# Reordering eighteen passes over six token units, with plain products in the first passes

## The chip, the cores and the metric

One Trainium2 chip, of which the kernel uses one core. A core has five engines that run beside each other, each through its own list of instructions in order: TensorE (PE) for matrix products, VectorE (DVE) and ScalarE (ACT) for element work, GpSimd (POOL), and SyncE (SP), whose list here only issues DMA transfers. The metric is device time in microseconds of the kernel's one core; lower is better.

## The reference

Attention with a mask that keeps the first `n_global` keys and the last `n_local` positions of each query, followed by a gated projection. Everything is float32, and the kernel has to match it to float32 accuracy.

```python
B, H, S, D = 4, 8, 768, 64          # n_global 8, n_local 96
scores = q @ k.T / sqrt(D)
keep = is_global | is_local
scores += -slope[h] * dist          # slope 2**-(h+1); dist = n_local for global keys
a = softmax(where(keep, scores, -1e9))
x = (a @ v)                         # reshaped to 3072 tokens x 512
out = ((x @ w_a) * (x @ w_b)) @ w_out   # w_a, w_b: 512 x 1536; w_out: 1536 x 512
```

## The kernel before, in words

**Units and granules.** The 3,072 tokens are cut into six units of 512 tokens (`NU`). Attention of a unit is four granules (`granule_ops`), one for each pair of heads. A granule loads a tile `qk` and a tile `vt`, has PE make the scores of its four blocks of 128 queries into PSUM banks `ps` (L544), lets DVE add the mask and take the maximum (L559), ACT the exponentials (L575), and DVE or ACT the division (L615, L612). The probabilities are then turned: for unit 0 by PE through the banks `pt` (`direct`), for the others by DVE in 32 x 32 squares into `tt` (L634), which goes by DMA to a DRAM tile `mir` and comes back in eight strided reads into `px` and `py` (`carry`). PE multiplies them with `vt` into a bank `pa` (L648), and ACT copies that to a quarter of the unit's tile `x` (tag `X`, one buffer).

**Passes.** The 1,536 columns of `w_a` and `w_b` are cut into six blocks of 256 (index `fp`, 0 to 5), and two blocks make a weight set: set A is `fp` 0 and 1, B is 2 and 3, C is 4 and 5. A pass is one set on one unit, and there are 18. `PASSES` (L48) orders them: A over units 0 to 5, B over 5 to 0, C over 0 to 5. A pass has two half passes, one for each `fp`. `project` makes the two products of a half pass by Strassen's scheme with seven products of 2 x 2 halves (`product`, L809, banks `al` and `ga`), each of 12 matmuls of 256 columns: a float32 factor is split in a high part `H` and a low part `L`, and three of the four cross products are taken. The products need seven forms of the weights (`FORMS`) and seven of `x` (`XFORMS`, made by `forms`): sums and differences of quarters, each then split by a cast and a subtraction (`split`, L299/L301 and L309). `back` (L907) multiplies the result, split into `hh` and `hl`, with the two blocks of `w_out` (`w_O`) into four PSUM banks `acc`, with 24 matmuls of 512 columns. The half passes overlap: PE does `back` of one between the products of later ones. When the unit changes, `evict` adds `acc` to what DRAM holds of that unit (`part`, through the tile `o`, three buffers) and stores it again, or to the output.

**Weights.** They arrive as 64-bit words and are made float32 by `to32`, six tiles for each `fp` (`wr<-wts`, then two ACT and four DVE instructions into `wm`). Set A is made straight into its SBUF slots (`direct`); sets B and C are made beside earlier passes, saved to DRAM (`dw<-wm`), and loaded and split into the slots when the set changes (`load_w`, `wl<-dw`). There are slots for one set only. The tile `x` of a unit is saved too (`dx<-x`) and loaded again for its later passes (`xl<-dx`).

**What sets the order.** Nothing here is placed by hand. Each instruction is an `Op` with a due time, the buffers it reads and writes, and a cost on each engine that may do it. `Schedule.order` runs a list schedule over these costs (earliest due time first among what is ready and has its buffers) and the instructions are emitted in the resulting order on each engine. `run` gives the due times: `times` are the starts of the passes, and the attention of a unit is spread from one and a half passes to half a pass ahead of its first use, so unit 1 has the first half of pass 0, and units 2 to 5 one pass each, up to the middle of pass 4. All DMAs go through SP's queue, in order.

## Time and profile before

| what | us |
|---|---|
| median of three runs (lowest, highest) | 773.75 (771.92, 776.95) |
| the profiled execution, its own time | 777.12 |
| its span (first to last instruction) | 775.3 |
| PE, DVE, ACT busy | 699.4, 579.0, 372.0 |
| moved by DMA | 149.55 MB, mean 193 GB/s |

In the profile's groups of instructions each row gives the line, the engine, the operation, the tile written and those read, and the count. The view by windows gives busy time of each engine in each stretch of the span, the share of full speed at which TensorE's clock was granted, the mean busy share of the 16 DMA engines and the rate. The view of instructions in order of time merges neighbours of a kind (`x12`); a row's duration contains the pipeline's depth, so the cost of one of several in a row is the distance between starts. In slices of a fortieth of the span (19.4 us), the DMA engines are at eight or nine tenths from the fifth to the nineteenth, and PE is at nine tenths without a break from the 20th to the 39th.

### The profile page before, as it was taken

The numbers are of one execution on the slowest core, as the hardware profiler recorded it, in microseconds if no ns is written. First come the engines' busy times: TensorE is split into PE (matmuls) and PEld (weight loads), VectorE is DVE, ScalarE is ACT, GpSimd is POOL, SyncE is SP. The second block draws the span as 40 slices with busy tenths as digits, with TensorE's granted clock in tenths as the row PEclk, the third lists the DMA queues.
The fourth block names the chain that finished last, engine by engine and source line by source line (L and its number), as shares of the span: only waits on it lengthen the run. The fifth ranks groups of instructions, "written<-read, shape, count | busy, mean of one in ns | idle before, by whom it ended". The sixth has DMA issues, their size and how long they took to land.

```text
span 775.3 us, 13998 instructions
## 1 busy us (share of the span) xinstructions
PE 699.4 (90%) x5104; PEld 633.3 (82%) x5104; DVE 579.0 (75%) x1610; ACT 372.0 (48%) x937; POOL 1.7 (0%) x8
## 2 busy tenths in 40 slices
PE   3875868989998979996999999999999999999993
PEld 3755756988887968886999999999999999999992
DVE  4799899988978767877998876757657567575551
ACT  2886686656567656654654623223434132232310
POOL 0000000000000000000000000000000000000000
PEclk9996999999999999999999999999999999999997
DMA  5664888999999989888574733314522232142031
GB/s 197 251 230 161 246 250 300 304 298 304 286 299 288 295 250 308 280 273 309 189 236 163 253 133 119 109 55 164 172 92 70 90 124 98 66 164 82 28 109 72
DMA packets 64093, 149.55 MB, mean 193 GB/s; under 512 B 7440, under 2 KB 26000, under 8 KB 61968
## 3 DMA queue, kind: packets, MB, share of 16 engines
q1 hardware_dynamic: 64016, 148.57, 57.3%
q8 instruction: 42, 0.69, 0.4%
q14 instruction: 35, 0.29, 0.1%
HBM read 100.31 MB, written 48.23 MB: 192 GB/s over the span
## 4 chain that ended last, share of the span: by engine, by line
PE 61%; DMA 19%; DVE 13%; ACT 3%; SPq 2%; issue 2%; DVEq 0%; ACTq 0%
PE al L809 20%; PE acc L907 20%; PE ga L809 15%; DMA mir<-tt 7%; DMA wr<-wts 5%; DMA qk<-qk 4%; PE pa L648 3%; PE ps L544 3%; DVE tt L634 2%; SPq L290 2%; DVE t L559 2%; DMA py<-mir 1%; ACT t L575 1%; DVE t L615 1%; DVE xf_T L309 1%
## 5 line engine op out<-in xcount | busy, mean ns | idle before, releaser
L907 PE MATMUL acc<-w_O,hh 128*128 128x512 f32 x576 | 197.9, 403 | 0.0
L809 PE MATMUL al<-xf_T,w_S 128*128 128x256 f32 x864 | 119.8, 288 | 12.1 <-ACT w_S L299 6.1
L907 PEld LDWEIGHTS acc<-w_O,hh 128*128 128x128 f32 x576 | 108.5, 188 | 23.1 <-issue 0.3
L809 PEld LDWEIGHTS al<-xf_T,w_S 128*128 128x128 f32 x864 | 110.9, 194 | 15.5 <-ACT s L299 7.0
L907 PE MATMUL acc<-w_O,hl 128*128 128x512 f32 x288 | 113.8, 395 | 0.2 <-DVE hl L309 0.2
L575 ACT ACTIVATE t<-t,sm 128x168 f32<-128x168 f32 x192 | 81.9, 428 | 50.4 <-DVE sm L559 50.2
L544 PE MATMUL ps<-qk 128*128 128x168 f32 x384 | 76.6, 329 | 28.5 <-DMA qk<-qk 18.3
L299 ACT COPY s<-al 128x512 f32<-128x512 f32 x71 | 41.6, 586 | 110.8 <-PE al L809 110.5
L544 PEld LDWEIGHTS ps<-qk 128*128 128x128 f32 x384 | 60.4, 199 | 38.3 <-DVE sm L559 15.0
L559 DVE CUSTOM_DVE_ANT_0 t<-ps,mask 128x168 f32<-128x168 f32 x192 | 57.0, 326 | 23.2 <-PE ps L544 23.1
L299 ACT CAST hh<-h 128x512 fp32r<-128x512 f32 x60 | 36.9, 619 | 63.5 <-DVE h L309 38.2
L809 PE MATMUL ga<-xf_B,w_A 128*128 128x256 f32 x432 | 59.8, 288 | 4.7 <-ACT xf_B L299 2.6
L838 DVE TENSOR_TENSOR s<-ga,s 128x512 f32<-128x512 f32 x72 | 49.6, 688 | 19.0 <-PE ga L809 18.5
L907 PEld LDWEIGHTS acc<-w_O,hl 128*128 128x128 f32 x288 | 54.3, 189 | 10.3 <-DVE hl L309 0.6
L809 PE MATMUL ga<-xf_B,w_S 128*128 128x256 f32 x432 | 58.1, 283 | 2.0 <-ACT s L299 1.8
L809 PEld LDWEIGHTS ga<-xf_B,w_A 128*128 128x128 f32 x432 | 55.2, 192 | 5.8 <-ACT xf_B L299 3.1
L809 PE MATMUL ga<-xf_T,w_S 128*128 128x256 f32 x432 | 58.5, 284 | 1.2 <-DVE w_S L309 1.2
L809 PEld LDWEIGHTS al<-xf_B,w_A 128*128 128x128 f32 x432 | 56.7, 192 | 3.2 <-DVE w_A L309 0.5
L809 PE MATMUL al<-xf_B,w_A 128*128 128x256 f32 x432 | 58.8, 285 | 0.3 <-DVE w_A L309 0.3
L809 PE MATMUL al<-xf_T,w_A 128*128 128x256 f32 x432 | 57.7, 282 | 0.4 <-DVE s L838 0.4
L809 PEld LDWEIGHTS ga<-xf_B,w_S 128*128 128x128 f32 x432 | 53.6, 188 | 3.4 <-ACT s L299 3.1
L809 PEld LDWEIGHTS al<-xf_T,w_A 128*128 128x128 f32 x432 | 54.4, 188 | 2.4 <-DVE s L838 1.4
(97 smaller groups left out, 1024.3 us busy)
## 6 DMA issues: line engine op xcount, KB each, us to landing
qk<-qk SPq DMA_DIRECT2D x24, 976.0 KB
wr<-wts SPq DMA_DIRECT2D x36, 512.0 KB
mir<-tt SPq DMA_DIRECT2D x20, 768.0 KB
vt<-vd SPq DMA_DIRECT2D x24, 512.0 KB
part<-o SPq DMA_DIRECT2D x40, 256.0 KB
xl<-dx SPq DMA_DIRECT2D x10, 1024.0 KB
o<-part SPq DMA_DIRECT2D x40, 256.0 KB
px<-mir SPq DMA_DIRECT2D x60, 128.0 KB
```

The lines of the kernel that those rows point to most:

```text
L290: lambda e: self.nc.sync.dma_start(out(), src()),
L299: self.nc.scalar.copy(out(), src())
L309: lambda e: self.nc.vector.tensor_tensor(out(), a(), b(), op=op),
L544: nc.tensor.matmul(ps[:, s * KW : s * KW + KW], qk[:, (2 * i + s) * P : (2 * i + s) * P + P], qk[:, k0 : k0 + KW], start=True, stop=True, ...
L559: lambda e, i=i, w=w, ps=ps, j=j, kind=kind: nc.vector.tensor_tensor_reduce(t[:, i, w], ps[:, w], self.mask[p][:, kind, w], -0.125, 3.0e38 ...
L575: lambda e, i=i, w=w, j=j: nc.scalar.activation(t[:, i, w], t[:, i, w], AF.Exp, bias=sm[:, 0, j : j + 1], scale=-1.0, accum_out=sm[:, 1, j ...
L615: nc.vector.tensor_scalar(flat()[:, j], flat()[:, j], sm[:, 3, j : j + 1], None, op0=ALU.mult)
L634: nc.vector.transpose(dst[:, s, b, e0 : e0 + n], src)
L648: nc.tensor.matmul(pa[64 * h : 64 * h + 64, i * P : i * P + P], vt[:lanes, v0 : v0 + 64], k[:, 2 * h : 2 * h + 2, :, i].rearrange("p g s k ...
L809: self.nc.tensor.matmul(bank[:, ab * HT : ab * HT + HT], w[:, a, (2 * ab + c) * P : (2 * ab + c) * P + P], x[:, b, c], start=first, stop=F ...
L838: lambda e: nc.vector.tensor_tensor(s[:, :], bank[:, :], s[:, :], op=ALU.add),
L907: self.nc.tensor.matmul(acc[i][:, :], a[:, rows], w[:, b], start=first and f == 0 and k == 0, stop=False, skip_group_check=True,)
```

## The change

- **Order of the passes.** A over units 0, 1, 2; B over 2, 1, 0; C over 0 to 5; B over 5, 4, 3; A over 3, 4, 5. The set changes four times in place of two, so B and A are loaded twice, and A's seven forms are made a second time from the input (`CONV`: `fp` 0 and 1 in passes 8 to 13) and saved to DRAM.
- **Attention.** Unit 1 keeps the first half of pass 0 and unit 2 its one pass; units 3, 4 and 5 have two and a half passes each, passes 2.5 to 10 (`SPANS`). Their result goes from the bank `pa` into the granule's own tile `vt` and from there to DRAM (`dx`), not into `X`, and `load_x` fetches it.
- **Plain products in passes 0 to 2** (`STD`, set A on units 0, 1, 2). `convert_plain` makes the four quarters and the two `w_out` blocks of set A without sums or differences; `plain_forms` splits the four quarters of `x` as they are; `project_plain` makes four products of 12 matmuls of 512 columns, the second of each two multiplied by DVE into `h`. The half passes of these three passes have 48 matmuls of 512 columns in place of 84 of 256.
- **Early slots.** The plain products leave six slots of set A unused; the first six forms of `fp` 2 are split into them while A is in use (`spread`, `slot`, `self.early`), and `load_w` skips these. The other forms of the first load of B rotate through the rest.
- **Start.** The two first `qk` tiles, the position table and the slopes are fetched ahead of the branch on the flag, into tiles outside the pools (`build`).
- **End.** The last pass loads its four old `part` blocks into the quarters of `X` and adds there (`close`), in place of the three `o` buffers.

The engines' lists show it at three places. The first is the end of SP's list, the last transfers of the program; `o` is the tile in which the old sum and `acc` are added, `part` the old sum in DRAM. Before:

```order
L290 DMA o_2_678611_8453<-part_2_349150_5078 128x512
L290 DMA out<-o_0_678611_8389 128x512
L290 DMA out<-o_1_678611_8393 128x512
L290 DMA out<-o_2_678611_8453 128x512
L290 DMA o_3_678611_8525<-part_3_349150_5104 128x512
L290 DMA out<-o_3_678611_8525 128x512
```

After, from the same kind of place:

```order
L301 DMA X<-part_2_542676_6922 128x512
L301 DMA X<-part_3_542676_6961 128x512
L301 DMA out<-o_0_666063_7959 128x512
L301 DMA out<-o_1_666063_7962 128x512
L301 DMA out<-o_2_666063_8024 128x512
L301 DMA o_3_666063_8258<-part_3_573523_7325 128x512
L301 DMA out<-o_3_666063_8258 128x512
L301 DMA out<-X 128x512 x4
```

The load of the fourth block stood behind the store of the last unit's third; now all four loads stand ahead of the previous unit's stores.

The second is PE's list at the first half pass, after the last granule of unit 0. Before:

```order
L809 MATMUL ga_0_624<-xf_B_40000_608,w_A_584 128x256 x12
L809 MATMUL al_0_546<-xf_T_40000_622,w_S_671 128x256 x12
L809 MATMUL al_0_546<-xf_T_40000_645,w_S_665 128x256 x12
L544 MATMUL ps_1_0_725<-qk_1_444 128x168 x2
L809 MATMUL ga_0_624<-xf_T_40000_480,w_S_658 128x256 x12
L809 MATMUL ga_0_624<-xf_B_40000_612,w_S_692 128x256 x12
```

After:

```order
L880 MATMUL al_0_0_593<-xp_0_313,w_A_0_499 128x512 x3
L880 MATMUL al_0_0_593<-xp_1_448,w_A_0_499 128x512 x3
L880 MATMUL al_0_0_593<-xp_2_565,w_A_0_539 128x512 x3
L880 MATMUL al_0_0_593<-xp_3_581,w_A_0_539 128x512 x3
L880 MATMUL ga_0_0_620<-xp_0_313,w_A_0_499 128x512 x3
L880 MATMUL ga_0_0_620<-xp_1_448,w_A_0_499 128x512 x3
```

The products read the quarters `xp` and `w_A` themselves; the sums and differences `xf_T` and `w_S` are gone from here.

The third is PE's list at the start of the pass of set B over unit 0, where the number after `al` or `ga` is that of the pass. Before (pass 11):

```order
L809 MATMUL al11_2_6242<-xf0_B11_450114_6093,w2_A11_288999_4087 128x256 x12
L809 MATMUL ga11_2_6255<-xf0_B21_450114_6111,w2_A12_288999_4182 128x256 x12
L809 MATMUL al11_2_6242<-xf0_T2_450114_6134,w2_S2_288999_4212 128x256 x12
L809 MATMUL ga11_2_6255<-xf0_T1_450114_6154,w2_S1_288999_4255 128x256 x12
L809 MATMUL al11_2_6242<-xf0_T3_450114_6193,w2_S3_288999_4321 128x256 x12
```

After (pass 5):

```order
L564 MATMUL ps4_0_0_3208<-qk0_78 128x168 x2
L861 MATMUL al5_2_3215<-xf0_B11_243959_3019,w2_A11_0_1236 128x256 x12
L861 MATMUL ga5_2_3231<-xf0_B21_243959_3091,w2_A12_0_1337 128x256 x12
L861 MATMUL al5_2_3215<-xf0_T2_243959_3111,w2_S2_0_1658 128x256 x12
L564 MATMUL ps4_0_1_3283<-qk0_78 128x168 x2
L861 MATMUL ga5_2_3231<-xf0_T1_243959_3137,w2_S1_0_1639 128x256 x12
L861 MATMUL al5_2_3215<-xf0_T3_243959_3270,w2_S3_0_1644 128x256 x12
L668 MATMUL pa3_3_3332<-px0_212,vt3_3_2749 64x128 x2
```

A pass that had products alone now has scores of unit 4 (`ps4_0`) and values of unit 3 (`pa3_3`) between them.

The diff, cut to its core:

```diff
-PASSES = [(0, u) for u in range(NU)] + [(1, u) for u in reversed(range(NU))] + [
-    (2, u) for u in range(NU)
-]
+ORDER = ((0, (0, 1, 2)), (1, (2, 1, 0)), (2, (0, 1, 2, 3, 4, 5)), (1, (5, 4, 3)), (0, (3, 4, 5)))
+PASSES = [(g, u) for g, us in ORDER for u in us]
+SPANS = {1: (0.0, 0.5), 2: (0.5, 1.5), 3: (2.5, 5.0), 4: (5.0, 7.5), 5: (7.5, 10.0)}
+NEAR = (0, 1, 2)
+CONV = {2: (0.8, 1.8), 3: (1.8, 2.8), 4: (3.2, 4.4), 5: (4.4, 5.6), 0: (8.0, 10.5), 1: (10.5, 13.0)}
+STD = tuple((0, u) for u in NEAR)
+PLAIN = ("A11", "A12", "A21", "A22")
+SLOT = {"A21": "S3"}
+XTAGS = ("B11", "B21", "B22", "T1")
...
+    def spread(self):
+        lead = FORMS[:6]
+        for k, name in enumerate(lead):
+            self.places[2, name] = f"w{k // 3}_" + ("S1", "S2", "S4")[k % 3]
+        rest = [(2, n) for n in ("A22", "O0", "O1")] + [(3, n) for n in FORMS + ("O0", "O1")]
+        free = [(f, n) for f in range(2) for n in ("A11", "A12", "S3", "A22", "O0", "O1")]
+        for (fp, name), (f, n) in zip(rest, free):
+            self.places[fp, name] = f"w{f}_{n}"
+        return [(2, name) for name in lead]
+
+    def slot(self, fp, name, due):
+        tag = self.places.get((fp, name)) or self.places.get((fp - 2, name))
+        tag = tag or f"w{fp % 2}_{SLOT.get(name, name)}"
+        self.places[fp, name] = tag
+        w = self.plan.buf(self.wp, [P, 2, CN], F32R, tag, f"w{fp}_{name}_{due:.0f}")
+        self.w[fp, name] = w
+        return w
+
     def wform(self, fp, name, due, src, direct):
-        if direct:
-            w = self.plan.buf(self.wp, [P, 2, CN], F32R, f"w{fp % 2}_{name}", f"w{fp}_{name}")
-            self.w[fp, name] = w
+        if direct or (fp, name) in self.early:
+            due += 0.0 if direct else 500.0
+            w = self.slot(fp, name, 0.0)
             self.split(due, lambda: src[:, :], w, lambda: w[:, 1], lambda: w[:, 0], CN, [src])
-            return
+            if direct:
+                return
...
+    def convert_plain(self, fp, due, step):
+        for i, name in enumerate(PLAIN + ("O0", "O1")):
+            m = self.to32(fp, i, due + i * step, "m" + (PLAIN + ("S1",))[i % 5])
+            self.wform(fp, name, due + i * step, m, True)
+
     def load_w(self, fp, due, step):
         for j, name in enumerate(FORMS + ("O0", "O1")):
+            if (fp, name) in self.early:
+                self.early.remove((fp, name))
+                continue
             at = due + j * step
-            w = self.plan.buf(
-                self.wp, [P, 2, CN], F32R, f"w{fp % 2}_{name}", f"w{fp}_{name}_{due:.0f}"
-            )
-            self.w[fp, name] = w
+            w = self.slot(fp, name, due)
...
+            self.copy(due + VLAG, lambda: x[:, p], lambda: pa[:, :], T, [pa], [(x, p)], psum=True)
+            return
+        self.copy(due + VLAG, lambda: vt[:, :T], lambda: pa[:, :], T, [pa], [vt], psum=True)
+        self.dma(
+            due + VLAG,
+            lambda: d[:, p * T : p * T + T],
+            lambda: vt[:, :T],
+            [vt],
+            [(d, p)],
+            T * 4 * P,
+        )
...
-        x = self.sbuf([P, NPAIR, T], F32, "X", f"x{u}", XBUFS)
+        if u in NEAR:
+            x = self.kept("X", f"x{u}")
+            for p in range(NPAIR):
+                self.granule_ops(u, p, t0 + (t1 - t0) * p / NPAIR, x)
+            return x
+        d = self.dram([P, NPAIR * T], F32, f"dx{u}")
+        self.xsaved[u] = d
         for p in range(NPAIR):
-            self.granule_ops(u, p, t0 + (t1 - t0) * p / NPAIR, x)
-        return x
+            self.granule_ops(u, p, t0 + (t1 - t0) * p / NPAIR, None, d)
...
+    def plain_forms(self, u, due, x):
+        done = []
+        for p in range(NPAIR):
+            f = self.sbuf([P, 2, T], F32R, "x_" + XTAGS[p], f"xp{u}_{p}")
+            self.split(
+                due,
+                lambda p=p: x[:, p],
+                f,
+                lambda f=f: f[:, 1],
+                lambda f=f: f[:, 0],
+                T,
+                [(x, p)],
+            )
+            done.append(f)
+        return done
...
+    def plain_product(self, due, bank, ws, k, x):
+        def emit(e):
+            for p in range(NPAIR):
+                w = ws[p // 2]
+                for a, b in ((0, 0), (0, 1), (1, 0)):
+                    self.nc.tensor.matmul(
+                        bank[:, :],
+                        w[:, a, (2 * k + p % 2) * P : (2 * k + p % 2) * P + P],
+                        x[p][:, b],
+                        start=p == 0 and a + b == 0,
+                        stop=False,
+                        skip_group_check=True,
+                    )
+
+        reads = [(b, h) for b in list(ws) + list(x) for h in "HL"]
+        self.plan.op(due, emit, reads, [bank], pe=12 * pe(T))
+
+    def project_plain(self, i, fp, due, x):
+        n = f"{i}_{fp}"
+        st = 12 * pe(T)
+        parts = []
+        for f in range(2):
+            ws = [self.w[fp, PLAIN[2 * f + c]] for c in range(2)]
+            al, ga = self.bank("al", f"al{n}_{f}"), self.bank("ga", f"ga{n}_{f}")
+            s = self.sbuf([P, T], F32, "s", f"s{n}_{f}", 3)
+            h = self.sbuf([P, T], F32, "h", f"h{n}_{f}", 2)
+            t = due + 2 * f * st
+            self.plain_product(t, al, ws, 0, x)
+            self.copy(
+                t + st, lambda s=s: s[:, :], lambda al=al: al[:, :], T, [al], [s], psum=True
+            )
+            self.plain_product(t + st, ga, ws, 1, x)
+            self.plan.op(
+                t + 2 * st,
+                lambda e, h=h, ga=ga, s=s: self.nc.vector.tensor_tensor(
+                    h[:, :], ga[:, :], s[:, :], op=ALU.mult
+                ),
+                [ga, s],
+                [(h, 0), (h, 1)],
+                dve=dve(T),
+            )
+            parts.append(self.cut(t + 2 * st, n, f, h))
+        return parts
...
+    def close(self, u, due, i, acc, o):
+        old = self.part[u, i]
+        self.dma(
+            due - 9000.0, lambda: o[:, i], lambda: old[:, :], [old], [(o, i)], 512 * 4 * P
+        )
+        self.plan.op(
+            due,
+            lambda e: self.nc.vector.tensor_tensor(o[:, i], acc[:, :], o[:, i], op=ALU.add),
+            [acc],
+            [(o, i)],
+            dve=dve(512),
+        )
+        r = u * T + i * P
+        self.dma(due, lambda: self.out[r : r + P], lambda: o[:, i], [(o, i)], [], 512 * 4 * P)
...
+        self.early = self.spread()
         self.masks()
         self.zeros()
         events = []
         x0 = self.attention(0, 0.0, START - ATT0)
-        self.convert(0, START - CONV0, STEP0, True)
+        self.convert_plain(0, START - CONV0, STEP0)
         self.save_x(0, START, x0)
-        xf = {0: self.forms(0, START - FORM0, x0)}
-        self.convert(1, START + CONV1, 2500.0, True)
-        live = None
+        xf = {0: self.plain_forms(0, START - FORM0, x0)}
+        self.convert_plain(1, START + CONV1, 2500.0)
         prev = None
         for i, (s, u) in enumerate(PASSES):
             t = times[i]
             if i and PASSES[i - 1][1] != u:
                 if events and events[0][0] == u:
-                    xf[u] = self.forms(u, t - 7000.0, events.pop(0)[1])
+                    x = events.pop(0)[1]
+                    xf[u] = (self.plain_forms if (s, u) in STD else self.forms)(u, t - 7000.0, x)
                 else:
                     xf[u] = self.load_x(u, t - 7000.0)
-            for v, (a, b) in span.items():
+            elif i and PASSES[i - 1] in STD and (s, u) not in STD:
+                xf[u] = self.forms(u, t - 7000.0, x)
...
+            for fp, (a, b) in CONV.items():
+                if i <= a < i + 1:
+                    self.convert(fp, at(a), (at(b) - at(a)) / 6, False)
...
+        tiles["X"] = cp.tile([P, NPAIR, T], F32, name="X")
+        width = 8 * KW
+        nc.sync.dma_start(tiles["qk0"], a["qk"][0, 0])
+        nc.sync.dma_start(
+            tiles["X"].rearrange("p a b -> p (a b)")[:, :width], a["pos"][:, :width]
+        )
+        nc.sync.dma_start(tiles["slope"], a["pos"][:, width:])
+        nc.sync.dma_start(tiles["qk1"], a["qk"][0, 1])
```

More of the change, by code (lines that the diff above doesn't have):

```diff
@@ L261, with __init__ @@
 class Fast:
-    def __init__(self, ctx, tc, a, out, nf, ident):
+    def __init__(self, ctx, tc, a, out, nf, ident, tiles=()):
         self.tc, self.nc = tc, tc.nc
@@ L265, in __init__ @@
         self.ctx = ctx
+        self.tiles = dict(tiles)
+        self.places = {}
         self.plan = Schedule()
@@ L451, in masks @@
         n = 2 * 2 * KW
[L452 to L453 removed]
+        full = self.kept("X", "tab")
+        self.slope = self.kept("slope", "slope")
         self.mask = [self.sbuf([P, 2, 2 * KW], F32, f"mask{p}", f"mask{p}") for p in range(1, 5)]
[L455 to L470 removed]
         part = lambda i: full[:, :].rearrange("p a b -> p (a b)")[:, i * n : i * n + n]
@@ L511, in zeros, with granule_ops @@
                 )
[L513 removed]
+    def granule_ops(self, u, p, due, x, d=None):
         nc, op = self.nc, self.plan.op
@@ L894, in project @@
         )
-        return [finish(due + 8 * st, f) for f in range(2)]
+        return [self.cut(due + 8 * st, n, f, h[f]) for f in range(2)]
     def back(self, fp, due, parts, acc, first):
@@ L922, in back, with evict @@
                 )
-    def evict(self, u, due, acc, first, last):
+    def evict(self, u, due, acc, first, last, final):
+        end = self.kept("X", f"end{due:.0f}") if final else None
         for i in range(4):
+            if final:
+                self.close(u, due, i, acc[i], end)
+                continue
             o = self.sbuf([P, 512], F32, "o", f"o{u}_{i}_{due:.0f}", 3)
@@ L960, in run @@
         fpt = 7 * 12 * pe(HT) + 24 * pe(512)
+        more = 12 * pe(HT)
         att = 4 * NPAIR * (2 * 620.0 + 530.0) / 2 * 1.0 + 600.0
-        first_use, last_use, seen = {}, {}, set()
+        last_use, seen = {}, set()
         for i, (s, u) in enumerate(PASSES):
-            first_use.setdefault(u, i)
             last_use[u] = i
         share = [0.0] * len(PASSES)
-        span = {}
-        prev = 0
-        for u in sorted(first_use, key=first_use.get):
-            if not first_use[u]:
-                continue
-            span[u] = None
-        for u in span:
-            span[u] = (max(first_use[u] - 1.0 - AHEAD, 0.0), first_use[u] - AHEAD)
-        for u, (a, b) in span.items():
+        for u, (a, b) in SPANS.items():
             for i in range(len(PASSES)):
@@ L979, in run @@
         for i in range(len(PASSES)):
-            times.append(times[-1] + 2 * fpt + share[i])
+            times.append(times[-1] + 2 * fpt + share[i] + (2 * more if PASSES[i] in STD else 0.0))
         def at(pos):
@@ L1026, in run @@
                 due = t + k * (times[i + 1] - t) / 2
-                parts = self.project(i, fp, due, xf[u])
+                plain = (s, u) in STD
+                parts = (self.project_plain if plain else self.project)(i, fp, due, xf[u])
                 if prev:
-                    prev(due + 84 * pe(HT))
+                    prev(due + (96 if plain else 84) * pe(HT))
                 over = k == 1 and (i + 1 == len(PASSES) or PASSES[i + 1][1] != u)
@@ L1034, in prev @@
                     if over:
-                        self.evict(u, d + 24 * pe(512), acc, u not in seen, i == last_use[u])
+                        self.evict(u, d + 24 * pe(512), acc, u not in seen, i == last_use[u], i + 1 == len(PASSES))
                         seen.add(u)
@@ L1253, in build @@
         nf, flag = build_counts(nc, cp, nv)
+        tiles = {
+            t: cp.tile([P, n], F32, name=t)
+            for t, n in (("qk0", QN + KN), ("qk1", QN + KN), ("slope", NPAIR))
+        }
+        tiles["X"] = cp.tile([P, NPAIR, T], F32, name="X")
[3 more added lines that the diff above has]
+            tiles["X"].rearrange("p a b -> p (a b)")[:, :width], a["pos"][:, :width]
+        )
+        nc.sync.dma_start(tiles["slope"], a["pos"][:, width:])
+        nc.sync.dma_start(tiles["qk1"], a["qk"][0, 1])
         fast = nc.values_load(flag[0:1, 0:1], min_val=0, max_val=1)
         inner = ctx.enter_context(ExitStack())
-        main = Fast(inner, tc, a, out, nf, ident)
+        main = Fast(inner, tc, a, out, nf, ident, tiles)
         with tc.If(fast > 0) as branch:
```

80 lines of the change are left out of this document (28 added, 52 removed).

## The prediction

> **What bounds the kernel now.** I read the head of the page first, then the windows between the places where the kernel changes its character, then the waits of PE in the stretch with the attention, then the end.
>
> ```profile
> span 775.3 us, 13998 instructions
> PE 699.4 (90%) x5104; PEld 633.3 (82%) x5104; DVE 579.0 (75%) x1610; ACT 372.0 (48%) x937; POOL 1.7 (0%) x8
> PE 61%; DMA 19%; DVE 13%; ACT 3%; SPq 2%; issue 2%; DVEq 0%; ACTq 0%
> ```
>
> PE is busy for 90% of the span, but the chain that ended last runs through it for 61% only, and through DMA and DVE for a third: some of the span is not PE's. The windows say where. Columns: busy time and instructions of each engine, granted clock, DMA share, rate.
>
> ```profile
> core 0: us, PE busy (x) PEld busy (x) DVE busy (x) ACT busy (x) POOL busy (x), PEclk, DMA share, GB/s
> 0.00:47.60 47.60, 29.29 (x237) 24.91 (x237) 32.15 (x159) 29.10 (x107) 1.75 (x8) 1.00 0.62 229
> 47.60:134.00 86.40, 61.70 (x447) 52.56 (x445) 81.50 (x266) 59.24 (x168) 0.00 (x0) 0.88 0.71 234
> 134.00:384.30 250.30, 230.28 (x1811) 205.67 (x1811) 206.80 (x721) 152.82 (x435) 0.00 (x0) 0.99 0.88 286
> 384.30:762.80 378.50, 378.07 (x2617) 350.20 (x2615) 257.79 (x466) 130.85 (x230) 0.00 (x0) 1.00 0.35 121
> 762.80:775.30 12.50, 0.04 (x1) 0.00 (x0) 0.75 (x2) 0.00 (x0) 0.00 (x0) 0.63 0.26 95
> ```
>
> The cuts are first products of a pass, found in PE's instructions in order of time:
>
> ```profile
> 133.99 1.69 PE L809 MATMUL al<-xf_B,w_A 128*128 128x256 f32 x12
> 384.28 1.57 PE L809 MATMUL al<-xf_B,w_A 128*128 128x256 f32 x12
> ```
>
> So: the start up to the first product; pass 0 (47.6 to 134.0), in which DVE is busy 81.5 of 86.4 us and sets the pace; passes 1 to 5 (to 384.3), with the DMA engines at 0.88; passes 6 to 17, in which PE never rests; and a tail of 12.5 us in which it does nothing. Only the second, third and last can give anything.
>
> **Prices.** From instructions and chain in order of time, one row for each kind:
>
> ```profile
> 747.40 1.41 PE al L809 x12
> 736.15 5.61 PE acc L907 x24
> 24.02 1.31 PE L544 MATMUL ps<-qk 128*128 128x168 f32 x8
> 34.40 0.44 PE L648 MATMUL pa<-px,vt 104*64 104x128 f32 x4
> 35.99 0.39 PE L648 MATMUL pa<-py,vt 128*64 128x128 f32 x4
> 60.37 0.69 DVE L309 TENSOR_TENSOR wm_S<-wm,wm 128x512 f32<-128x512 f32 x1
> 60.97 0.69 DVE L309 TENSOR_TENSOR w_A<-wm,w_A 128x512 fp32r<-128x512 f32 x1
> 65.78 0.43 DVE L343 TENSOR_SCALAR wm<-wm 128x512 f32<-128x512 f32 x1
> 745.42 0.43 DVE L309 TENSOR_TENSOR h<-s 128x256 f32<-128x256 f32 x1
> ```
>
> A matmul of 256 columns takes 1.41 / 12 = 0.1175 us, one of 512 columns 5.61 / 24 = 0.234. The scores of two blocks take 1.31 with the pipeline's end, 0.57 a block; the values of a granule run from 34.40 to 36.2, 1.8. A two-operand DVE instruction of 512 columns starts 0.60 after its neighbour; the two kinds that last 0.43 in place of 0.69 I step at 0.34.
>
> PE's own work follows by counting its list. Passes 1 to 5 hold 840 matmuls of 256 columns (98.7), 228 of 512 (53.3), 16 sets of values (28.8) and 57 blocks of scores (32.5): 213.3 of 250.3 us, so 37.0 are waiting and switching, with some 15 granules. Passes 6 to 17 hold 2,016 (236.9) and 600 (140.3): 377.2 of 378.5, so 1.3 is lost without attention. The second calibrates the prices; the first is the loss in dispute.
>
> **The start and pass 0.** Up to the first product of pass 1, DVE's list has 46 two-operand instructions of 512 columns on weights, forms and products before and 25 after. Those on weights go from 26 (for each of two `fp`, 4 sums and 9 splits) to 13, those on `x` from 14 to 8, and 6 additions in `project` become 4 products: 21 x 0.60 = 12.6 us less, and 8 products of 256 columns less (8 x 0.34 = 2.7). Two more weights of set B are converted here (two-operand 4 x 0.60, one-operand 5 x 0.34: 4.1), and casts and a few attention instructions add 1.3. Net 9.9 us less of the engine that sets the pace. The bounds: 0, if the waits between the engines keep their length, and 13.7, if the waiting in this stretch goes too (47.6 + 86.4 less the table's arrival at 9.8 less 110.5 of DVE work counted in these steps); I take 9.9, since DVE is at 94% there. PE's dearer products (48 x 0.234 = 11.2 in place of 84 x 0.1175 = 9.9 for a half pass) cost 1.35 twice in this pass, hidden by DVE.
>
> The table from which DVE makes the masks is fetched ahead of the branch:
>
> ```profile
> 0.76 0.40 SPq L1250 DMA_DIRECT2D nv<-ns  x1
> 5.51 0.34 SPq L290 DMA_DIRECT2D tab<-pos  x1
> 9.79 0.57 DVE L476 TENSOR_SCALAR tab<-tab,nf 128x672 f32<-128x672 f32 x1 [5.26 <-DMA tab<-pos]
> ```
>
> Its issue moves from 5.5 to about 1.6, but it now follows 976 KB of `qk`, and DVE cannot use it before the branch. Between 0 and 4 us gained, I take 2. Pass 1 then starts at 134.0 - 9.9 - 2 = 122.1.
>
> **Passes 1 to 9.** These hold the rest of the attention now. PE's list has 1,176 matmuls of 256 columns (138.2), 600 of 512 (140.4: 408 in `back`, 192 in the four half passes with plain products, of which 4 x 1.35 = 5.4 are new), 15 sets of values (27.0) and 56 blocks of scores (31.9): 337.5 us. What is lost beside it? The waits of PE in passes 1 to 5, longest sums first:
>
> ```profile
> PE ps L544 <- DMA qk<-qk: 4.7, 3, 3.4
> PE ps L544 <- DVE sm L559: 3.7, 6, 1.4
> PE pa L648 <- DMA py<-mir: 3.5, 5, 1.3
> PE al L809 <- ACT s L299: 3.2, 4, 1.5
> PE pa L648 <- DMA px<-mir: 1.5, 1, 1.5
> ```
>
> Of the 37.0 us lost, 4.7 + 3.5 + 1.5 = 9.7 are waits for a DMA, in the stretch where the engines that move data are nearly full. The rest goes with the granules: each puts scores and values between products, and waits a little for DVE and ACT. The same 15 granules over nine passes in place of five should keep the second part, 37.0 - 9.7 = 27, and lose most of the first. Bounds: 3 (the loss of passes 6 to 17 for nine passes), and 58 (the loss grows with PE's work: 37.0 / 213.3 x 337.5). I take 27, as the granules' number is what stays the same.
>
> The bytes are a second limit on this stretch. SP's list has, with the sizes of the page's DMA issues,
>
> ```profile
> qk<-qk SPq DMA_DIRECT2D x24, 976.0 KB
> wr<-wts SPq DMA_DIRECT2D x36, 512.0 KB
> mir<-tt SPq DMA_DIRECT2D x20, 768.0 KB
> vt<-vd SPq DMA_DIRECT2D x24, 512.0 KB
> part<-o SPq DMA_DIRECT2D x40, 256.0 KB
> px<-mir SPq DMA_DIRECT2D x60, 128.0 KB
> ```
>
> 13 `qk` (13.0 MB), 33 `wr` (17.3), 15 `mir` (11.8) and their way back (10.3), 15 `vt` (7.9), 138 transfers of 256 KB for weights, sums and results (36.2) and 7 of 1 MB (7.3): 103.8 MB. At the 286 GB/s of passes 1 to 5 that takes 363 us, within a microsecond of 337.5 + 27. So the stretch ends at 122.1 + 364.5 = 486.6 by either reading, and there is no room in it: all that the spread takes out per microsecond, the second conversion and the extra loads of weights put back. By the Trainium skill ("DMA: Bandwidth & Descriptors", Specifications) one core can draw some 358 GB/s from its memory, and 103.8 MB would be an estimated 290 us, well under PE's work. No window of this trace shows that rate, so I keep the row's.
>
> **Passes 10 to 17.** 1,344 matmuls of 256 columns (157.9), 408 of 512 (95.4) and one last set of values (1.8) are 255.1; with 1 us lost, 256.1. The loads of B and A in here are like the load of C in passes 11 and 12 before, which stands in the window with 1.3 us lost. They end at 742.7. The two evictions that are gone (the unit now stays at four changes of set, at two before) were 8 additions of DVE and 16 transfers; they are in the counts of bytes, and PE did not wait for them.
>
> **The tail.** The chain at the end:
>
> ```profile
> 761.49 3.53 DMA out<-o
> 765.08 2.58 DMA o<-part
> 767.86 0.69 DVE o L938
> ```
>
> The fourth block's old sum has no free `o` until a store has landed, so store, load and addition follow each other. With four quarters of `X` loaded ahead, the last addition starts at about 762.9, when the last matmul ends: 767.9 - 762.9 = 5.0 less, and the tail is 7.5. The last store stays. Nothing hides this part, and nothing is late in its place.
>
> **The sum.** 122.1 + 364.5 + 256.1 + 7.5 = 750.2 against a span of 775.3: 25.1 less. The profiled execution took 777.12 us, 3.4 above the median of the three runs; taken off the median, 773.75 - 25.1 = 748.6, **about 748.5 us** (3.3% less).
>
> **Rivals.** *No change.* The loss goes with time, not with granules: PE's list is served in order, every transfer of a granule stands in SP's one queue behind all the extra weights, and 0.17 of PE's work is lost in passes 1 to 9 as in 1 to 5. Then 58 in place of 27 gives 748.5 + 31 = 779.5. For it: the DMA engines stay as full as they were. Against: the waits for DMA are only a quarter of the loss.
>
> *Slower.* One mechanism: the first load of set B. Block `fp` 3 is converted up to 2.8 passes and used from 3.5, and each of its nine forms goes to DRAM and back first. One such trip is 3.53 for a store, 2.58 for a load and 1.2 for cast and subtraction, 7.3; nine in series are 66, of which 0.7 pass, 22 us, is there. That would be 44 more, 792; it decides the sign once a form's own share of the trip exceeds (25 + 22) / 9 = 5.2 us. Against it: set B is saved and loaded in pass 5 before too, and none of PE's waits in that stretch names a weight. The Trainium skill ("DMA: Bandwidth & Descriptors", Bandwidth, Measured) speaks for it, with the rule to batch transfers to 1 MiB or more for three quarters of the peak, as most of what is added is 256 KB; by that rule the later loads would be late too. The windows do not bear it out: passes 6 to 17, with transfers of 256 KB and 1 MB alone, move 121 GB/s at a share of 0.35, 346 for a full share, where the attention's stretch has 286 / 0.88 = 325.
>
> *Faster still.* With the work spread, the loss falls to 5 and the start gains its upper bounds, 4 more: 748.5 - 26 = 722.5. For it: passes 6 to 17 run without loss beside DVE at 68%. Against: the bytes; it needs 103.8 / 342.5, some 303 GB/s throughout.
>
> **How the numbers follow.** A measurement of this kernel can tell about 1% from no change. Forecast 0.70 (its own range 734 to 765, 27 of loss give or take 12 and the start give or take 4), no change 0.10, slower 0.06, faster still 0.14. The range 726 to 772 leaves out about half of the fast rival, half of no change and all of the slow one, under 0.2. Faster by over 1% (below 766): 0.66 + 0.14 = 0.80; within 1%: 0.14; slower: 0.06.
>
> **What would show it.** Pass 1 starts near 122 with DVE still over 90% before it; passes 1 to 9 take about 365 us at a DMA share of 0.85 to 0.9 and some 285 GB/s; passes 10 to 17 about 256 with PE full; the chain's end has no `o<-part` after the last matmul. I am wrong if a weight (`w_A`, `w_S`, `w_O`) appears high among PE's waits, if passes 1 to 9 take over 385 us or under 350, or if the two loads of A and B after pass 10 open gaps on PE.

## The result, and the profile after

The changed kernel takes 746.8 us (median of four runs, 745.9 to 750.8) against 774.4 for the kernel before on the same chip: a ratio of 0.965 with an interval of 0.961 to 0.970, so 27.6 us or 3.6% less. The profiled execution took 750.77 us, 4.0 above its median; that of the kernel before stood 3.4 above its own. Runs over 1.5% above the fastest of the same kernel are left out of the medians and ratios below. The head of its page and the same stretches of its windows as before:

```profile
span 748.9 us, 13720 instructions
PE 705.6 (94%) x4888; PEld 632.9 (85%) x4888; DVE 580.1 (77%) x1601; ACT 390.3 (52%) x980; POOL 1.8 (0%) x8
PE 50%; DVE 21%; DMA 19%; ACT 6%; issue 2%; SPq 1%; DVEq 0%; ACTq 0%
```

```profile
core 0: us, PE busy (x) PEld busy (x) DVE busy (x) ACT busy (x) POOL busy (x), PEclk, DMA share, GB/s
0.00:50.00 50.00, 33.02 (x272) 29.10 (x273) 36.98 (x170) 33.21 (x123) 1.75 (x8) 0.93 0.66 234
50.00:121.30 71.30, 62.88 (x355) 49.79 (x354) 65.09 (x237) 51.59 (x151) 0.00 (x0) 0.90 0.90 293
121.30:485.20 363.90, 351.78 (x2483) 314.77 (x2482) 317.87 (x910) 217.95 (x556) 0.00 (x0) 0.99 0.87 289
485.20:742.90 257.70, 257.70 (x1785) 239.24 (x1783) 159.15 (x286) 87.59 (x154) 0.00 (x0) 1.00 0.31 102
742.90:748.90 6.00, 0.25 (x2) 0.00 (x0) 0.98 (x2) 0.00 (x0) 0.00 (x0) 0.86 0.46 168
```

The cuts are again the first products of pass 0, 1 and 10, and the end of the last matmul. Pass 0 is shorter (71.3 us in place of 86.4), and the DMA engines, at 0.71 there before, are now at 0.90: the stretch in which data is scarce begins a pass earlier. Passes 1 to 9 run at 0.87 and 289 GB/s on average; single passes lie between 0.71 and 0.94, and between 233 and 331 GB/s. From pass 10 on PE never rests. PE is busy 94% of the span, but the chain that ended last runs through it for only half: for the first 485 us it changes engine again and again.

The longest waits of PE in passes 1 to 9 (line, tile, what it waited for: sum, times, longest), and the chain at the end:

```profile
PE al L861 <- ACT s L310: 3.8, 3, 2.2
PE pa L668 <- DMA py<-mir: 2.8, 7, 0.6
PE ps L564 <- DVE sm L579: 2.4, 4, 1.0
PE pa L668 <- DMA px<-mir: 1.8, 1, 1.8
PE ga L861 <- DVE s L945: 1.2, 2, 0.8
```

```profile
734.78 8.38 PE acc L1003 x36
743.16 0.02 issue
743.19 0.69 DVE X L1064
```

No weight stands among the waits, and the wait for `qk` (4.7 us before) is gone; the named DMA waits add up to 4.6 in place of 9.7. At the end no load follows the last matmul: the addition starts with it.

### The profile page after: what moved, and what is told of

Read it like the earlier page. It is cut to its first block, busy times and chain, and to the rows that moved or that the text cites. A ratio compares the mean times of both kernels' runs of the same rounds, so it can differ in the third digit from the quotient of the medians.

```text
span 748.9 us, 13720 instructions
## 1 busy us (share of the span) xinstructions
PE 705.6 (94%) x4888; PEld 632.9 (85%) x4888; DVE 580.1 (77%) x1601; ACT 390.3 (52%) x980; POOL 1.8 (0%) x8
## 4 chain that ended last, share of the span: by engine, by line
PE 50%; DVE 21%; DMA 19%; ACT 6%; issue 2%; SPq 1%; DVEq 0%; ACTq 0%
PE acc L1003 16%; PE al L861 15%; PE ga L861 11%; DMA wr<-wts 9%; PE ps L564 3%; DVE tt L654 2%; DMA qk<-qk 2%; PE pa L668 2%; DVE t L579 2%; DMA py<-mir 2%; ACT t L595 2%; DVE wm L389 2%; DVE wm L372 2%; DMA wl_A<-dw_A 2%; PE ga L880 1%
## 5 line engine op out<-in xcount | busy, mean ns | idle before, releaser
L861 PE MATMUL al<-xf_T,w_S 128*128 128x256 f32 x720 | 97.5, 285 | 3.8 <-ACT s L310 3.8
L861 PEld LDWEIGHTS al<-xf_T,w_S 128*128 128x128 f32 x720 | 91.7, 190 | 5.8 <-ACT s L310 4.4
L320 DVE TENSOR_TENSOR hl<-h,hh 128x512 fp32r<-128x512 f32 x72 | 48.6, 683 | 8.9 <-ACT hh L310 8.6
L861 PEld LDWEIGHTS al<-xf_B,w_A 128*128 128x128 f32 x360 | 46.7, 189 | 2.5 <-issue 0.3
L861 PE MATMUL al<-xf_B,w_A 128*128 128x256 f32 x360 | 48.5, 284 | 0.0
L861 PE MATMUL al<-xf_T,w_A 128*128 128x256 f32 x360 | 48.3, 284 | 0.0
L861 PE MATMUL ga<-xf_B,w_A 128*128 128x256 f32 x360 | 48.2, 284 | 0.0
L861 PE MATMUL ga<-xf_B,w_S 128*128 128x256 f32 x360 | 48.2, 283 | 0.0
L861 PEld LDWEIGHTS ga<-xf_T,w_S 128*128 128x128 f32 x360 | 45.8, 190 | 1.9 <-DVE s L945 1.6
L654 DVE STREAM_TRANSPOSE tt<-t 128x256 f32<-128x256 f32 (+1 forms) x160 | 45.9, 344 | 0.7 <-ACT t L632 0.5
```

The source lines that it names most:

```text
L320: lambda e: self.nc.vector.tensor_tensor(out(), a(), b(), op=op),
L654: nc.vector.transpose(dst[:, s, b, e0 : e0 + n], src)
L861: self.nc.tensor.matmul(bank[:, ab * HT : ab * HT + HT], w[:, a, (2 * ab + c) * P : (2 * ab + c) * P + P], x[:, b, c], start=first, stop=F ...
```

## The experiments

Medians; the kernel before ran beside each at 772.3 to 775.4. A ratio is to the kernel before, with its 95% interval in brackets. The kernel before moves by 3 us between these groups of runs, so differences between experiments are no finer than that. Where a theory is named after the bytes or after the granules, it is the one of these two that explains the 26 us lost in passes 1 to 9.

**1. The start and the end alone.** Old order, old spans and seven products everywhere; only the early fetches and `close` remain.

```diff
-ORDER = ((0, (0, 1, 2)), (1, (2, 1, 0)), (2, (0, 1, 2, 3, 4, 5)), (1, (5, 4, 3)), (0, (3, 4, 5)))
+ORDER = ((0, (0, 1, 2, 3, 4, 5)), (1, (5, 4, 3, 2, 1, 0)), (2, (0, 1, 2, 3, 4, 5)))
-SPANS = {1: (0.0, 0.5), 2: (0.5, 1.5), 3: (2.5, 5.0), 4: (5.0, 7.5), 5: (7.5, 10.0)}
-NEAR = (0, 1, 2)
+SPANS = {1: (0.0, 0.5), 2: (0.5, 1.5), 3: (1.5, 2.5), 4: (2.5, 3.5), 5: (3.5, 4.5)}
+NEAR = (0, 1, 2, 3, 4, 5)
-STD = tuple((0, u) for u in NEAR)
+STD = ()
```

> The old order of passes, the old spans of attention and the old seven products everywhere, with only the two ends of the change: the first tiles fetched ahead of the branch and the last pass adding in the quarters of X. Theory (each part of the change gives its own piece): the tail falls from 12.5 to about 6 to 7.5 us and the start gains 1 to 2, so 773.75 - 7 = 767, give or take 2, with passes 1 to 5 still about 250 us. Rival (the ends are hidden or given back, the gain is all from the order): 773 or more.

Measured 768.9, ratio 0.993 [0.991, 0.996]: 5 us, within what was expected, where the terms of the prediction were 5.0 for the end and 2 for the start. The windows (start and pass 0, passes 1 to 5, passes 6 to 17, tail) divide it otherwise:

```profile
0.00:128.30 128.30, 89.55 (x629) 77.67 (x629) 107.82 (x404) 84.50 (x264) 1.75 (x8) 0.88 0.70 228
128.30:380.60 252.30, 236.05 (x1861) 212.07 (x1862) 214.11 (x744) 154.09 (x440) 0.00 (x0) 0.99 0.89 291
380.60:762.10 381.50, 380.88 (x2616) 354.17 (x2615) 258.68 (x467) 130.25 (x229) 0.00 (x0) 1.00 0.37 120
762.10:770.70 8.60, 0.43 (x2) 0.00 (x0) 1.15 (x2) 0.00 (x0) 0.00 (x0) 0.80 0.34 126
```

Pass 1 begins 5.7 us earlier than at 134.0, and the tail is 3.9 shorter. Of these 9.6, passes 1 to 5 give back 2.0 and passes 6 to 17 3.0; the latter is a longer step of the matmuls, to which experiments 11 and 12 come back. Of the 5.7, DVE's first use of the table (8.8 in place of 9.8) explains 1.0; the first product of pass 0 comes 1.7 earlier, at 45.9, and the other 4.0 fall in pass 0 itself, for a reason that this run does not name.

**2. No plain products.** The changed kernel with seven products in the first passes too, without the early slots.

```diff
-STD = tuple((0, u) for u in NEAR)
+STD = ()
-        self.early = self.spread()
+        self.early = []
-        self.convert_plain(0, START - CONV0, STEP0)
+        self.convert(0, START - CONV0, STEP0, True)
-            xf = {0: self.plain_forms(0, START - FORM0, x0)}
+            xf = {0: self.forms(0, START - FORM0, x0)}
```

> The changed kernel with its new order and spans, but the seven products and seven forms also in passes 0 to 2, and no early slots. Theory (the plain products pay through DVE in pass 0): pass 1 starts about 10 us later, near 131, passes 1 and 2 have 5.4 us less PE work but more DVE work, so 747 + 5 to 10 = 752 to 757. Rival (the dearer products cost what they save, and the order alone gives the gain): 747 or less.

Measured 773.0, ratio 0.999 [0.997, 1.002]. A miss by some 18 us (752 to 757 was expected): without the plain products the new order and the spread give nothing, not even what the ends alone give. Its windows up to pass 1 and over passes 1 to 9:

```profile
0.00:122.90 122.90, 84.95 (x629) 73.13 (x629) 107.47 (x404) 84.42 (x264) 1.75 (x8) 0.90 0.72 238
122.90:505.40 382.50, 362.70 (x2693) 328.63 (x2694) 336.57 (x961) 228.81 (x588) 0.00 (x0) 0.98 0.86 288
```

Pass 1 starts only 1.6 us later than in the profile of the changed kernel. But less stands done by then: PE has been busy 85.0 us in place of 33.0 + 62.9 = 95.9, and 122.9 x 238 = 29.2 MB have moved in place of 50.0 x 234 + 71.3 x 293 = 32.6. Passes 1 to 9 then take 18.6 us more. Counted from the lists as in the prediction, PE's work in them is 3.7 more and the bytes are 108.7 MB in place of 103.8; 4.9 MB at 288 GB/s would be 17 us if every byte counted, which experiment 8 tests.

**3. The attention not spread.** Plain products and new order, but units 3 to 5 in one pass each again.

```diff
-SPANS = {1: (0.0, 0.5), 2: (0.5, 1.5), 3: (2.5, 5.0), 4: (5.0, 7.5), 5: (7.5, 10.0)}
+SPANS = {1: (0.0, 0.5), 2: (0.5, 1.5), 3: (1.5, 2.5), 4: (2.5, 3.5), 5: (3.5, 4.5)}
```

> The changed kernel with the attention of units 3, 4 and 5 in one pass each again, passes 1.5 to 4.5, the order of passes and all else as in the change. Theory (the loss goes with the granules, a quarter of it with full DMA engines): passes 1 to 9 lose about 37 in place of 26 us, so 747 + 10 = 757. Bytes as the limit: the bytes of 15 granules and of the weights of B come in passes 1 to 4, some 85 to 95 MB, at 290 to 310 GB/s near 300 us for what has 200 us of PE work; the rest of passes 5 to 9 is 155, so the stretch takes some 430 in place of 364 and the kernel 800 or more. Rival (spreading does nothing): 747, within 3.

Measured 789.7, ratio 1.020 [1.016, 1.023], 43 us over the changed kernel and slower than before. Passes 1 to 4:

```profile
116.70:359.50 242.80, 210.14 (x1414) 177.57 (x1413) 196.62 (x691) 137.04 (x395) 0.00 (x0) 0.92 0.92 301
```

The list counts 71.3 MB and 185 us of PE's work here, so 57 us are lost. The measured time lies between the 757 of the granules' theory and the 800 of the bytes', nearer the latter. That 71.3 MB at 301 GB/s make 237 of the 242.8 us proves nothing by itself, since the rate is bytes over time; for the bytes speaks the share of 0.92, the highest of the stretches of several passes here. The clock counts as well: it was granted at 0.92, and PE was busy 210 us for its 185 of work.

**4. Fewer bytes, same work.** The changed kernel with the loads of `qk` after the first two cut to their first 128 columns. PE, DVE and ACT do the same instructions on other data, and 12.1 of the 103.8 MB in passes 1 to 9 are gone (and 8.4 before them).

```diff
-                lambda: qk[:, :],
-                lambda: self.a["qk"][u, p],
+                lambda: qk[:, :P],
+                lambda: self.a["qk"][u, p, :, :P],
```

> The changed kernel in the same order, with each load of a granule's qk after the first two cut to its first 128 columns of 1,952, so the scores of later granules use what the tile held before; 12.1 MB less in passes 1 to 9. Bytes as the limit of the stretch: 12.1 MB at 289 GB/s, 42 us less, 705. Loss by granules and PE's work as the limit: only waits for DMA go, under 5 us, and a little at the start, so 741 to 747.

Measured 739.9, ratio 0.956 [0.953, 0.960]: 7 us, where the bytes alone would have freed 42; the other theory, 741 to 747, is missed by 1. Passes 1 to 9:

```profile
115.60:472.00 356.40, 347.06 (x2482) 311.15 (x2482) 317.08 (x910) 217.32 (x556) 0.00 (x0) 1.00 0.80 262
```

The rate falls to 262 GB/s and the share to 0.80, so bytes bind less, and still 356.4 - 337.5 = 18.9 us are lost. PE's busy time is 4.7 us less for the same instructions, at a clock of 1.00 in place of 0.99.

**5. More bytes, same work.** Every `qk` after the first two is read a second time, into a DRAM tile that nothing uses: 13.0 MB more in passes 1 to 9 and 9.0 before them.

```diff
+            ex = self.dram([P, QN + KN], F32, "ex" + n)
...
+                nc.sync.dma_start(ex[:, :], self.a["qk"][u, p])
```

> The changed kernel in the same order, with a second read of the same granule's qk, into a DRAM tile that nothing uses, issued behind each load of qk after the first two: 12.7 MB more in passes 1 to 9 and 9 MB more before. If bytes do not set the pace as they stand but stand close (cutting 12.1 MB gave 7 us), the stretch cannot go below 116.5 MB at 290 to 310 GB/s, 376 to 402 us in place of 364, and pass 0 grows too: 765 to 795. If bytes have room (granules and PE alone count): under 755.

Measured 789.4, ratio 1.020 [1.015, 1.025], 42.6 us over the changed kernel. Passes 1 to 9:

```profile
127.50:527.30 399.80, 364.86 (x2484) 325.93 (x2483) 318.59 (x911) 218.62 (x557) 0.00 (x0) 0.95 0.88 300
```

The 42.6 us are the price of all 22.0 MB. In passes 1 to 9, 13.0 MB at 300 GB/s would be 43 us, and 399.80 - 363.90 = 35.9 were measured: upward most bytes count, downward (experiment 4) few do. The changed kernel stands at the corner where both limits meet. Of the 35.9, 364.86 - 351.78 = 13.1 lie in PE's busy time, for the same instructions: the clock was granted at 0.95 in place of 0.99, and 0.04 of 399.8 us is 16. So the price of late bytes is not waiting alone.

**6. The same cut in the kernel before.** The loads of `qk` from the third granule on are cut to 128 columns, 12.1 MB in passes 1 to 5.

```diff
+        qw = QN + KN if g < KBUFS else P
-            lambda: qk[:, :],
-            lambda: self.a["qk"][u, p],
+            lambda: qk[:, :qw],
+            lambda: self.a["qk"][u, p, :, :qw],
```

> The kernel before in its own order, with each load of qk after the first two cut to 128 columns: 12.1 MB less of 70.0 in passes 1 to 5. Theory of the prediction (of the 37 us lost there, 9.7 wait for DMA and the rest goes with the granules): 774 - 10 = 764, or 760 with a little of pass 0. Bytes as the limit of that stretch (70.0 MB at 286 GB/s): the 37 us lost go, up to PE's work and the 5% that granules lose elsewhere, 774 - 25 to 37 = 737 to 749.

Measured 758.0, ratio 0.978 [0.973, 0.983]: 17 us, between the theories and nearer the first. Passes 1 to 5, to be laid beside the 250.30 of before:

```profile
134.00:366.90 232.90, 224.16 (x1810) 204.13 (x1809) 205.84 (x719) 151.84 (x434) 0.00 (x0) 0.99 0.80 255
```

17.4 of the 37.0 us lost there went with the bytes, not 9.7. What is left, 232.9 - 213.3 = 19.6, is near what experiment 4 left with some 15 granules over nine passes (18.9). The cut relieves the queue and also shortens the one load that the scores wait for; these runs do not tell the two apart.

**7. No attention for units 3 to 5.** The changed kernel with twelve granules left out; those units use the `x` of unit 0.

```diff
-        d = self.dram([P, NPAIR * T], F32, f"dx{u}")
-        self.xsaved[u] = d
-        for p in range(NPAIR):
-            self.granule_ops(u, p, t0 + (t1 - t0) * p / NPAIR, None, d)
+        self.xsaved[u] = self.xsaved[0]
```

> The changed kernel without the attention of units 3, 4 and 5, which take unit 0's result from DRAM: 12 granules fewer in passes 3 to 10. Loss by granules: each costs 4.1 of PE's work and 1.8 of loss, 12 x 5.9 = 71, so 676. Loss in proportion to PE's work (8% of it): PE's work falls by 49 and the loss by 4, so 694. If the loss is something else in these passes (the change of set, conversions), it also stays: 694 or more.

Measured 681.6, ratio 0.881 [0.876, 0.885]: 65.2 us for twelve granules, 5.4 each, where the work of one on PE is 1.8 + 4 x 0.57 = 4.1. So 1.3 is lost beside each, bytes included; the time lies between the two theories (676 and 694), nearer the first. Passes 3 to 9 are almost bare, 220.8 us for 216.7 of PE's work:

```profile
196.10:416.90 220.80, 219.62 (x1513) 203.67 (x1513) 195.80 (x368) 106.26 (x188) 0.00 (x0) 1.00 0.61 204
```

**8. Fewer bytes without plain products.** Experiment 2 with the cut of experiment 4.

> The changed order and spans with seven products everywhere (which took 773), and each load of qk after the first two cut to 128 columns. If its extra 26 us over the change are DVE's 10 at the start and the rest bytes (108.7 MB fall due in its passes 1 to 9, against 103.8), the cut gives back more than the 7 us that it gave the change: its 42 us of loss fall to the 20 or so that both kernels kept with the cut, so 773 - 20 = 753. If the rest is waiting at the change of set or other work of the seven products, the cut gives 7 as in the change: 766.

Measured 758.4, ratio 0.984 [0.976, 0.991], between the 753 and the 766. Passes 1 to 9:

```profile
122.60:489.50 366.90, 355.80 (x2692) 325.04 (x2693) 334.86 (x961) 229.01 (x588) 0.00 (x0) 0.99 0.82 264
```

Against experiment 4 these passes take 10.5 us more; with all bytes it was 18.6. So 8.1 of the 18.6 were bytes that fall later when the start is slow. Of the 18.5 us that stay between the two kernels (758.4 - 739.9), 7.0 is the start (122.6 against 115.6) and 10.5 these passes: 3.7 of PE's work left behind and 6.8 more loss, whose cause these runs do not name.

**9. No early slots.** Plain products kept, the slots not rotated.

```diff
-        self.early = self.spread()
+        self.early = []
```

> The changed kernel with plain products, but without the early forms of fp 2 and the rotation of slots: all of set B goes through DRAM and is loaded at the change of set. The variant with seven products took 26 us more than the change, of which about 10 is DVE's work at the start (theory of the prediction), and lost 11 us more in pass 2. If the early slots are what hides the first change of set: pass 2 and 3 lose 10 us more, 755 to 760. If the plain products alone do it (less DVE work, slots free sooner): 747, within 3.

Inconclusive: 747.4, 750.1, 758.8 and 759.2 lie too far apart for an interval. The profiled one (750.1) started pass 10 at 484.2; the changed kernel did so at 485.2 in its profile, and at 481.2 and 481.8 in experiments 11 and 12, which have the same instructions. What the early slots give stays open.

**10. Spread further.** Units 3 to 5 up to pass 10.6, the second conversion of set A from pass 10.2 on.

```diff
-SPANS = {1: (0.0, 0.5), 2: (0.5, 1.5), 3: (2.5, 5.0), 4: (5.0, 7.5), 5: (7.5, 10.0)}
+SPANS = {1: (0.0, 0.5), 2: (0.5, 1.5), 3: (2.5, 5.2), 4: (5.2, 7.9), 5: (7.9, 10.6)}
-CONV = {2: (0.8, 1.8), 3: (1.8, 2.8), 4: (3.2, 4.4), 5: (4.4, 5.6), 0: (8.0, 10.5), 1: (10.5, 13.0)}
+CONV = {2: (0.8, 1.8), 3: (1.8, 2.8), 4: (3.2, 4.4), 5: (4.4, 5.6), 0: (10.2, 11.8), 1: (11.8, 13.4)}
```

> The changed kernel with the attention of units 3 to 5 spread up to 10.6 passes in place of 10, and the second conversion of set A moved from 8 to 13 to 10.2 to 13.4 passes: some 3 to 4 MB less in passes 3 to 9. If the stretch stands at the corner of bytes and PE's work, it gains 3 to 6 us: 741 to 744. If bytes have no part in it: 747, within 2.

Measured 747.5, ratio 0.967 [0.960, 0.973]: no gain. But the edit did not do what was expected of it: passes 1 to 9 (116.4 to 484.8) moved 368.4 us x 287 GB/s = 105.7 MB, in place of 363.9 x 289 = 105.2 in the changed kernel, and 33 loads `wr` were issued in them in both. The new due times took hardly a transfer out of these passes, so this run does not test whether more spreading would help.

**11 and 12. Where the operands lie.** In passes 10 to 17, without any wait, 12 matmuls of 256 columns took 1.44 us after and 1.42 before. In the built programs the weight slots begin 64 bytes past a multiple of 128 after and in experiment 1 (its step is 119.6 ns too), 32 past one before and in experiment 6 (118.0 too). Two kernels shift them by unused tiles; every instruction is the same. The first:

```diff
         tiles["X"] = cp.tile([P, NPAIR, T], F32, name="X")
+        cp.tile([P, 8], F32, name="pad")
```

> The changed kernel with an unused tile of 32 bytes per partition ahead of the weight slots: every instruction is the same, and all that lies behind it in the memory (weight slots, forms of x) sits 32 bytes further on. Theory (the step of a 256-column matmul depends on where its operands lie: 119.5 ns in the changed kernel and in those derived from it, whose weight slots start at a multiple of 64 bytes, 117.9 ns in the kernel before and in the one with its scores cut, whose slots start 32 bytes past one): with the slots 32 bytes past a multiple of 64 the step falls to 117.9 ns, passes 10 to 17 take 1.344 x 1.6 = 2.2 us less (255.5 in place of 257.7) and the kernel about 743 us. Rival (the step goes with something else, such as the order of the instructions or what else runs): 119.5 ns and 747 us.

The second has 24 in place of 8, and 8 more ahead of the pool `s`.

> The same with 96 bytes ahead of the weight slots and 32 more ahead of the forms of x, so that both lie at the same place within 128 bytes as in the kernel before (slots 32 past a multiple of 128, forms 64 past one); every instruction is the same. If the step depends on the place of slots and forms against each other, or on the place within 128 bytes, this run alone falls to 117.9 ns and about 743 us; if on the slots' place within 64 bytes, both do; if the rival holds, neither.

Measured 748.7 (ratio 0.971 [0.967, 0.976]) and 746.5 (0.968 [0.962, 0.975]); the runs scatter from 741.8 to 751.7, so the totals do not tell 2 us. The chain in order of time does, in pass 14, of the changed kernel, the first and the second:

```profile
612.46 1.44 PE al L861 x12
622.54 5.58 PE acc L1003 x24
```

```profile
608.47 1.44 PE al L861 x12
618.54 5.58 PE acc L1003 x24
```

```profile
608.25 1.41 PE al L863 x12
618.11 5.61 PE acc L1005 x24
```

The second alone has the step of the kernel before: over the 924 steps in passes 11 to 16 the mean is 117.9 ns, against 119.6 in the other two. Its matmuls of 512 columns, in turn, take 233.7 in place of 232.3. A pass of passes 11 to 16 takes 31.01 in place of 31.26 us. So the theory of the first run missed: the slots' place within 64 bytes alone is not it. Slots 32 bytes past a multiple of 128 are one reading; slots and forms of `x` 32 bytes apart within 64 is another, which these runs do not separate. It is no version that can be told to beat the changed kernel by its times.

## Why the prediction was right, and where a step was not

**The start.** Forecast 122.1, measured 121.3. DVE's busy time up to pass 1 fell from 32.15 + 81.50 to 36.98 + 65.09, 11.6 less, where I had 9.9; for the table I had 2 and it gave 1.3:

```profile
1.68 0.42 SPq L1367 DMA_DIRECT2D X<-pos  x1
8.47 0.57 DVE L495 TENSOR_SCALAR X<-X,nf 128x672 f32<-128x672 f32 x1 [3.72 <-DMA X<-pos]
```

The sum came out, its parts did not. Experiment 1 has 5.7 us of the start without new order or plain products, where I had 2; with the new order and spread (experiment 2) pass 1 begins another 5.4 earlier, at 122.9, and of DVE's 11.6 us some 6 are gone by then. The plain products, which were to bring 9.9, bring 1.6 against the profile shown and 4 to 6.5 against the others below. That these pieces add up to my 12 is luck.

What failed besides is the mark that I used. I priced the plain products by when pass 1 begins, 9.9 us, and hid the rest behind DVE. Experiment 2 begins pass 1 nearly as early without them (its DVE is busy 107.5 us by then, in place of 113.7 before), and takes 26 us more: a slow start leaves PE's work and bytes behind, and they arrive in passes where the DMA engines are already full. The profile shown is on the late side, too: in experiments 9 to 12, with the same plain start, pass 1 begins at 116.4 to 118.7.

**Passes 1 to 9.** Forecast 364.5, measured 363.9, with 289 GB/s where I had 286. The sum was right, the parts of its loss were not. I split the 37.0 us lost before into 9.7 of DMA waits, which the spread would remove, and 27 that stay with the granules. Experiments 4 and 6 put the part that stays at 18.9 and 19.6, about the same in both kernels, and the bytes' part at 17.4 before. A wait that is named after DVE or ACT can still begin with late data; of the 17.4, 230.28 - 224.16 = 6.1 lies in PE's busy time, where no wait is named at all. Of the bytes' part the change removed 10 and left 7.5 (363.9 - 356.4), and 18.9 + 7.5 makes the 26.4 that I had, as 27, for granules alone: again a right sum of wrong parts. The second limit, 103.8 MB at 286 GB/s, was the sounder of my two readings on the side above (experiments 3 and 5), and no limit on the side below (experiment 4). Nor is 286 a ceiling: pass 4 alone ran at 331 GB/s, at a share of 0.93.

The rate that the Trainium skill gives for one core ("DMA: Bandwidth & Descriptors", Specifications), some 358 GB/s, was not reached by any pass of the changed kernel, and keeping the row's 286 for the average was right. But it is no ceiling here: the start of experiment 5, with its second reads, went above it for 30 us, at a share of 0.95:

```profile
3.00:33.00 30.00, 21.38 (x158) 19.24 (x159) 22.17 (x116) 17.55 (x69) 1.04 (x2) 1.00 0.95 373
```

**Passes 10 to 17.** Forecast 256.1, measured 257.7. The loss of 1 us was not there at all; the price was mis-sized: 1,344 x (119.6 - 117.5) = 2.8 more, and 408 x (233.8 - 232.3) = 0.6 less. The two later loads of A and B opened no gap.

**The tail.** Forecast 7.5, measured 6.0: the fourth block's load is gone, as told. The last addition ends 5.0 us before the end of the span, where it was 6.8 before and 7.4 in experiment 1; the tail is short by that as well, which I had not forecast.

**The rivals.** The slow one fell: no weight stands among PE's waits, although set B is used from 3.5 passes on. So the rule against transfers under 1 MiB ("DMA: Bandwidth & Descriptors" of the Trainium skill, Bandwidth, Measured) did not decide here. The stretch that I set against it was not as I said: passes 6 to 17 before also hold seven loads `wr` of 512 KB. Passes 10 to 17 after hold none, and move 102 GB/s at a share of 0.31, 329 for a full share. The faster one, a loss of 5, is out while the granules are there: passes 3 to 9 of experiment 7, with them gone, lose 4. The first, no change, is what the kernel does without the plain products, but not by the reason given, that 0.17 of PE's work is lost: experiment 2 loses 41 us of 341, or 0.12.

**The parts together.** The ends give 5 of the 27 us by themselves. New order and spread without plain products give nothing beyond them, and new order and plain products without the spread make the kernel 16 slower than before. Only together do they give the other 22. Plain products under the old order were not tried, and experiment 2 leaves out the early slots with them. Of the 26 that the two are worth, experiment 8 puts 8 down to bytes, 7 to the start and 4 to PE's work left behind; 7 stay open.

## What to carry to other kernels

A stretch near both PE's and the DMA engines' limit has to be priced by each limit and by bytes from both sides: here, in the same nine passes, 13.0 MB more cost 36 us and 12.1 MB less gave 7.5. The named DMA waits measure the bytes' part badly (9.7 against 17.4 us); cutting the bytes at the same instructions measures it better. And a run that moves due times has to be checked in its trace for whether the transfers moved (experiment 10). A start is worth more than the moment at which the next stage begins: count what it leaves undone for a stage that has no room.

## What was not expected of the hardware

Kernels with seven products in pass 0 spend 17 to 21 us there at half clock, after PE has starved (in the 3.4 us before it, the kernel before has PE busy for 0.8). The windows of before in pass 0, cut where the granted clock changes:

```profile
47.60:56.00 8.40, 5.38 (x54) 4.41 (x53) 8.12 (x23) 8.08 (x24) 0.00 (x0) 1.00 0.53 169
56.00:73.10 17.10, 9.94 (x43) 9.06 (x42) 16.36 (x40) 9.04 (x18) 0.00 (x0) 0.50 0.53 194
```

Experiments 2, 6 and 8 show the same stretch at the same length, experiment 1 one of 20.5; the changed kernel has 3.4 us of it there, and 6.8 and 3.4 later in the pass. By the Trainium skill ("TensorE: Matmul & The Clock Gate", Part 1) the gate works in windows of about 3.4 us, and 17.1 is five of them, in which PE is busy 58%. DVE is busy 16.4 of the 17.1 us, so what the half clock costs by itself in this stretch no run here shows.

The step of a matmul depends on where its operands lie (experiments 11 and 12): 119.6 or 117.9 ns at 256 columns, and the other way round at 512, 232.3 or 233.7.
